# Attention backward for one query row: four stores of dV rewritten from 128 partitions to 124 and 4

## The chip, the core and the metric

The kernel runs on one core of a Trainium2 chip. The core has five engines with instruction streams of their own (PE for matrix products, DVE and ACT for elementwise work, POOL, and SP, which here only issues transfers) and sixteen DMA engines that carry all bytes between HBM and the on-chip memory of 128 partitions. The metric is device time in microseconds for one launch. Before the change it was 663.56 us, the median of 9 runs (662.63 to 664.14). Lower is better.

## What is computed

One query row per head attends to 8192 keys, for 32 heads of width 128. Output and the three gradients are wanted, all in bfloat16:

```python
B, H, Sq, Skv, Dh = 1, 32, 1, 8192, 128
scores = jnp.einsum('bhqd,bhkd->bhqk', q, k) * Dh ** -0.5
attn   = softmax(scores, axis=-1)
out    = jnp.einsum('bhqk,bhkd->bhqd', attn, v)
out, vjp = jax.vjp(forward, q, k, v); dq, dk, dv = vjp(grad_out)
```

K and V are 2 MB per head and are read once; dK and dV are 2 MB per head and are written once. Each row of dK is a number times q, and each row of dV is a probability times the gradient of the output, so both are outer products. In all 128 MB are read and 128 MB written.

## The kernel before

**Tiles.** A head's 8192 rows lie on 128 partitions with 64 consecutive rows each: partition p holds rows 64p to 64p + 63, 16 KB in one piece both in HBM and on chip. `rows_of(x, h, c, parts)` is the c-th of `parts` pieces of those 64 rows on every partition, and `slots(X, c, parts)` the same piece of a tile. A half (parts = 2) is 128 partitions of 8 KB, a quarter (parts = 4) 128 partitions of 4 KB. K has three buffers of a whole head, V two, and each of the two gradient tiles G two.

**Loop.** Iteration h works on head h and finishes head h - 1 beside it. For head h: four block transposes of K on DVE (line 142) and the scores on PE (line 154); maximum, exponential and sum (lines 262 to 289); then, on V, transposes on PE (line 180), their copies on ACT (line 182), the output product (line 197) and the products with the gradient (line 192). At its end `outer(h, "dv", r)` for r = 0 to 3 makes a quarter of dV each on DVE. For head h - 1 the same function makes the quarters of dK, spread over the iteration, and the gradient of q comes from K again (line 197).

**Stores.** `outer` multiplies on DVE (line 207) and, after every second quarter, issues the store of a half (line 215). For the last head it stores each quarter.

**Order of the transfers.** All transfers are issued by SP, and everything in the loop stands in an order written out by hand. In iterations 1 to 29 SP issues, in this order: V of the next head (line 81), the first half of dK of the previous head (line 215), K of the head after next (line 75), the second half of that dK, and the two halves of dV of this head: six transfers and 8 MB. The first K and V and the last V come in quarters.

**Waits.** SP waits before an issue for whatever the transfer needs: the tile's maker for a store, the last reader of the buffer for a load. It also waits for the landing of the transfer eight issues before, since eight completion semaphores are used in turn. Every transfer of 128 partitions is cut over the sixteen DMA engines, eight partitions on each, and it has landed when the last engine has finished its part.

Of the kernel before, what the change touches and what calls it, by code (L numbers as in the profile page):

```python
# [18 lines left out]
V_BUFS = 2  # L19
NST = 2  # L20
QD = 32


@with_exitstack
def kernel(
# [11 lines left out]
    nc = tc.nc  # L37
    P = 128
# [3 lines left out]
    NCH = NT // CH  # L42
    NQ = P // QD
    assert NCH == 4 and NQ == 4
    W = D // 2
    NB = W // QD
    scale = float(D) ** -0.5
# [15 lines left out]
    def rows_of(x, h, c, parts):  # L63
        L = NT // parts
        return x[0, h].rearrange("(p n) d -> p n d", p=P)[:, c * L:(c + 1) * L, :]

    def slots(X, c, parts):
        L = NT // parts
        return X[:, c * L:(c + 1) * L, :]
# [28 lines left out]
    nc.vector.reduce_sum(in_quad[:], ident[:].rearrange("p (a i) -> p a i", a=NQ), axis=AX.X)  # L98
    lane = consts.tile([P, QD], F32)
    nc.vector.reduce_sum(lane[:], ident[:].rearrange("p (a i) -> p i a", a=NQ), axis=AX.X)  # L100
# [3 lines left out]
    for w in range(NB):  # L104
        for e2 in range(2):
            four = consts.tile([H, NQ, QD], BF16, tag=f"four{w}{e2}")
            nc.vector.tensor_copy(
                four[:], rows[:, 0, :].rearrange("h (w j e) -> h w e j", w=NB, e=2)[:, w, e2:e2 + 1, :]
                .to_broadcast([H, NQ, QD]))
            tp = psT.tile([P, CH, P], BF16, tag="T")  # L110
# [26 lines left out]
    def k_blocks(h, u):  # L137


        if u == 0:  # L140
            XK[h] = ktpool.tile([P, CH, NB, NCH, QD], F32, tag="XK", name="XK_sb")
        nc.vector.transpose(XK[h][:, :, :, u, :],  # L142
# [57 lines left out]
    def outer(h, which, r):  # L200
        x = st[h]
        if r == 0:
            x[which] = gpool.tile([P, NT, D], BF16, tag=which, name="G_" + which)
        G, dst = x[which], out_2 if which == "dk" else out_3
        rep, row = x["ds"] if which == "dk" else x["p"], x["qd"][:, 0 if which == "dk" else 1, :]
        Q = NT // 4
        nc.vector.tensor_tensor(  # L207
            slots(G, r, 4).rearrange("p n (a b) -> p n a b", b=R),
            slots(rep, r, 4).unsqueeze(2).to_broadcast([P, Q, D // R, R]),
            row.rearrange("p (a b) -> p a b", b=R).unsqueeze(1).to_broadcast([P, Q, D // R, R]),  # L210
            op=ALU.mult)
        parts = 4 if h == H - 1 else NST
        if r % (4 // parts) == 4 // parts - 1:
            c = r // (4 // parts)
            nc.sync.dma_start(rows_of(dst, h, c, parts), slots(G, c, parts))

    def rows_bc(h):
        x = st[h]
# [21 lines left out]
    for h in range(H + 1):  # L240
# [8 lines left out]
        if h > 0:  # L249
            ds_of(p_)  # L250
            outer(p_, "dk", 0)
            dq_of(p_, 0)
# [3 lines left out]
        if h > 0:  # L256
            dq_of(p_, 1)
            outer(p_, "dk", 1)
# [11 lines left out]
        if h > 0:  # L270
            outer(p_, "dk", 2)
# [77 lines left out]
```

## Time and profile before

| | before |
|---|---|
| median of 9 runs | 663.56 us |
| the profiled execution | 663.56 us, of which its span 661.8 us |
| PE, PE weight load, DVE, ACT busy | 79%, 74%, 78%, 28% of the span |
| DMA | 408 GB/s on average; HBM read 134.23 MB, written 134.23 MB |
| stores of dV | 62 of 1024 KB (25.6 us from issue to landing), 4 of 512 KB |
| stores of dK | 62 of 1024 KB (27.8 us), 4 of 512 KB |
| loads of V | 30 of 2048 KB (28.2 us), 8 of 512 KB |

The span runs from the first to the last instruction of one execution; times in the chain of waits and in the windows count from its start. In the chain, each line is a start, a duration and the work that the next piece of the chain waited for. A transfer's duration there is from its issue to its landing, with the time that it waits behind others. The queue lines give packets, megabytes and the share of the sixteen engines' time. Queue 1 carries the kernel's transfers; queues 8 and 14 bring instructions.

### The profile page before, as it was taken

The numbers are of one execution on the slowest core, as the hardware profiler recorded it, in microseconds if no ns is written. First come the engines' busy times: TensorE is split into PE (matmuls) and PEld (weight loads), VectorE is DVE, ScalarE is ACT, GpSimd is POOL, SyncE is SP. The second block draws the span as 40 slices with busy tenths as digits, with TensorE's granted clock in tenths as the row PEclk, the third lists the DMA queues.
The fourth block names the chain that finished last, engine by engine and source line by source line (L and its number), as shares of the span: only waits on it lengthen the run. The fifth ranks groups of instructions, "written<-read, shape, count | busy, mean of one in ns | idle before, by whom it ended". The sixth has DMA issues, their size and how long they took to land.

```text
span 661.8 us, 21100 instructions
## 1 busy us (share of the span) xinstructions
PE 523.1 (79%) x9705; PEld 488.0 (74%) x9705; DVE 513.4 (78%) x664; ACT 182.2 (28%) x321; POOL 0.7 (0%) x6
## 2 busy tenths in 40 slices
PE   2888888789888778878778787788877888778880
PEld 1888788689887777877668776687766887667870
DVE  5789889788897797777977779777788776886862
ACT  0333223232333222232222322223222322222330
POOL 0000000000000000000000000000000000000000
PEclk9955556656565566655666556666566665566665
DMA  8999999999999999999999999999999999999783
GB/s 328 414 424 427 427 421 429 415 424 428 428 423 426 426 423 428 426 426 422 427 426 425 425 429 425 423 426 419 408 423 413 419 415 406 414 417 405 295 356 144
DMA packets 29800, 269.83 MB, mean 408 GB/s; under 512 B 3472, under 2 KB 3472, under 8 KB 6032
## 3 DMA queue, kind: packets, MB, share of 16 engines
q1 hardware_dynamic: 29712, 268.48, 97.2%
q8 instruction: 76, 1.25, 0.7%
q14 instruction: 12, 0.10, 0.0%
HBM read 134.23 MB, written 134.23 MB: 406 GB/s over the span
## 4 chain that ended last, share of the span: by engine, by line
DMA 70%; PE 21%; DVE 3%; ACT 2%; issue 1%; SPq 0%; ACTq 0%
DMA Kt<-in_k_dram 26%; DMA Vt<-in_v_dram 25%; DMA out_dram<-G_dv 19%; PE T_ps L180 9%; PE s_ps L154 2%; PE m_ps L197 2%; PE dp_ps L197 2%; PE dp_ps L192 2%; ACT XT_sb L182 1%; DVE XK_sb L142 1%; PE m_ps L267 1%; PE m_ps L280 1%; DVE G_dk L207 1%; ACT e L279 1%; PE s_ps L170 1%
## 5 line engine op out<-in xcount | busy, mean ns | idle before, releaser
L180 PE MATMUL T_ps<-ident_f,Vt 128*128 128x128 f32 x1024 | 240.0, 413 | 30.7 <-DMA Vt<-in_v_dram 30.7
L180 PEld LDWEIGHTS T_ps<-ident_f,Vt 128*128 128x128 f32 x1024 | 198.1, 221 | 31.9 <-issue 29.5
L142 DVE STREAM_TRANSPOSE XK_sb<-Kt 128x1024 f32<-128x1024 f32 x128 | 148.1, 1213 | 71.3 <-DMA Kt<-in_k_dram 71.3
L182 ACT COPY XT_sb<-T_ps 128x1024 f32<-128x1024 f32 x128 | 129.6, 1013 | 196.1 <-PE T_ps L180 196.1
L207 DVE TENSOR_TENSOR G_dk<-ds_rep,qd 128x2048 bf16<-128x2048 bf16 x128 | 155.7, 1218 | 1.1
L207 DVE TENSOR_TENSOR G_dv<-p_rep,qd 128x2048 bf16<-128x2048 bf16 x128 | 148.2, 1219 | 9.0 <-ACT p_rep L289 8.8
L192 PEld LDWEIGHTS <-XT_sb 128*128 128x128 bf16 x2048 | 76.6, 105 | 30.2 <-ACT XT_sb L182 27.5
L192 PE MATMUL dp_ps<-do_blk,XT_sb 128*128 128x2 bf16 x2048 | 72.9, 165 | 24.7 <-ACT XT_sb L182 24.7
L197 PE MATMUL dp_ps<-ds_rep,Kt 128*128 128x1 bf16 x2048 | 64.8, 165 | 6.5 <-issue 5.9
L197 PEld LDWEIGHTS <-Kt 128*128 128x128 bf16 x2048 | 60.0, 104 | 12.3 <-issue 12.2
L154 PE MATMUL s_ps<-q_blk,XK_sb 128*128 128x4 bf16 x2048 | 57.9, 167 | 10.4 <-DVE pdt L228 7.7
L154 PEld LDWEIGHTS <-XK_sb 128*128 128x128 bf16 x2048 | 55.4, 100 | 12.3 <-DVE pdt L228 9.4
L197 PEld LDWEIGHTS <-Vt 128*128 128x128 bf16 x2048 | 62.6, 106 | 2.0
L197 PE MATMUL m_ps<-p_rep,Vt 128*128 128x1 bf16 x2048 | 60.5, 166 | 0.0
L280 PEld LDWEIGHTS m_ps<-rs,ones_f 128*128 128x128 f32 x64 | 16.0, 310 | 48.6 <-ACT e L279 48.6
L280 PE MATMUL m_ps<-rs,ones_f 128*128 128x1 f32 x64 | 18.7, 362 | 39.2 <-ACT e L279 39.2
L238 ACT COPY dq_all<-dp_ps 128x1 f32<-128x1 f32 x32 | 5.1, 159 | 159.4 <-PE dp_ps L197 159.4
L276 DVE TENSOR_REDUCE nbias<-m_ps 128x1 f32<-128x128 f32 x32 | 9.3, 292 | 24.2 <-ACT qd L223 24.2
L230 DVE SCALAR_TENSOR_TENSOR ds_rep<-dp_ps,pdt,p_s 128x256 bf16<-128x256 f32 x32 | 15.5, 484 | 15.5 <-PE dp_ps L192 13.3
L267 PE MATMUL m_ps<-diag,ones_f 128*128 128x128 f32 x64 | 25.5, 499 | 2.2 <-issue 1.5
L289 ACT ACTIVATE p_rep<-e,rinv 128x256 bf16<-128x256 f32 x32 | 16.3, 508 | 30.2 <-DVE rinv L287 30.2
L223 ACT CAST qd<-m_ps 128x256 bf16<-128x256 f32 x32 | 11.9, 372 | 44.6 <-PE m_ps L219 44.6
(44 smaller groups left out, 161.4 us busy)
## 6 DMA issues: line engine op xcount, KB each, us to landing
Kt<-in_k_dram SPq DMA_DIRECT2D x31, 2048.0 KB, 27.8
out_dram<-G_dv SPq DMA_DIRECT2D x62, 1024.0 KB, 25.6
out_dram<-G_dk SPq DMA_DIRECT2D x62, 1024.0 KB, 27.8
Vt<-in_v_dram SPq DMA_DIRECT2D x30, 2048.0 KB, 28.2
Vt<-in_v_dram SPq DMA_DIRECT2D x8, 512.0 KB, 13.9
Kt<-in_k_dram SPq DMA_DIRECT2D x4, 512.0 KB, 5.4
out_dram<-G_dv SPq DMA_DIRECT2D x4, 512.0 KB, 16.8
out_dram<-G_dk SPq DMA_DIRECT2D x4, 512.0 KB, 11.1
```

Of the source, the lines that this page charges most:

```text
L142: nc.vector.transpose(XK[h][:, :, :, u, :], slots(Kt[h], u, NCH).rearrange("p g d -> p (g d)").bitcast(F32).rearrange("p (g w j) -> p g w ...
L154: nc.tensor.matmul(out[:, g, :], lhsT=cols[:, g, c // 2, c % 2], rhs=q_blk[:, h, c, :], start=(c == 0), stop=(c == 2 * NB - 1), skip_group ...
L180: nc.tensor.transpose(T_ps[:, i, :], words[:, m * P:(m + 1) * P], ident_f[:])
L182: nc.scalar.copy(X[:], T_ps[:])
L192: nc.tensor.matmul(st[h]["dp"][:, n:n + 2], lhsT=X[:, i, e2, :], rhs=do_blk[:, h, e2, :], start=(e2 == 0), stop=(e2 == 1), skip_group_chec ...
L197: nc.tensor.matmul(out_col, lhsT=Xt[:, n, :], rhs=rep[:, n, 0:1], start=(n == 0), stop=(n == NT - 1), skip_group_check=True)
L207: nc.vector.tensor_tensor(slots(G, r, 4).rearrange("p n (a b) -> p n a b", b=R), slots(rep, r, 4).unsqueeze(2).to_broadcast([P, Q, D // R, ...
L223: nc.scalar.copy(x["qd"][:].rearrange("p a d -> p (a d)"), x["m"][:, 256:512])
L230: nc.vector.scalar_tensor_tensor(out=x["ds"][:], in0=x["dp"][:, 0:NT].unsqueeze(2).to_broadcast([P, NT, R]), scalar=pdt[:], in1=x["p_s"][: ...
L267: nc.tensor.matmul(x["m"][:, 128:256], lhsT=ones_f[:], rhs=diag[:], start=True, stop=True, skip_group_check=True)
L280: nc.tensor.matmul(x["m"][:, 0:1], lhsT=ones_f[:], rhs=rs[:], start=True, stop=True, skip_group_check=True)
L289: nc.scalar.activation(x["p"][:], e[:].unsqueeze(2).to_broadcast([P, NT, R]), ACT.Copy, scale=rinv[:])
```

## The change

One branch is added to `outer`, for the second half of dV of heads 7, 13, 19 and 25. In place of one store of a half, three are issued: the third quarter on 128 partitions, then the last quarter of partitions 0 to 123, then the last quarter of partitions 124 to 127. The bytes and their places are the same. The products on DVE and their order are the same. According to its description, the last quarter's bytes move on DMA engines 0 to 3 alone.

```diff
+SHIFTED = (7, 13, 19, 25)
...
         parts = 4 if h == H - 1 else NST
         if r % (4 // parts) == 4 // parts - 1:
             c = r // (4 // parts)
-            nc.sync.dma_start(rows_of(dst, h, c, parts), slots(G, c, parts))
+            if which == "dv" and h in SHIFTED and c == 1:
+
+                nc.sync.dma_start(rows_of(dst, h, 2, 4), slots(G, 2, 4))
+                for lo, hi in ((0, P - 4), (P - 4, P)):
+                    nc.sync.dma_start(rows_of(dst, h, 3, 4)[lo:hi], slots(G, 3, 4)[lo:hi])
+            else:
+                nc.sync.dma_start(rows_of(dst, h, c, parts), slots(G, c, parts))
```

## The prediction

> **What bounds the kernel now.** I read the page first, then the chain of waits, then windows of the end, then the single packet records.
>
> ```profile
> span 661.8 us, 21100 instructions
> ...
> q1 hardware_dynamic: 29712, 268.48, 97.2%
> q8 instruction: 76, 1.25, 0.7%
> ...
> DMA 70%; PE 21%; DVE 3%; ACT 2%; issue 1%; SPq 0%; ACTq 0%
> ...
> Kt<-in_k_dram SPq DMA_DIRECT2D x31, 2048.0 KB, 27.8
> ```
>
> The sixteen DMA engines are busy 97.2% of the span, and a 2 MB load that needs 4.9 us at 427 GB/s lands 27.8 us after its issue: it waits behind other transfers. The chain of waits, in order of time, shows where that ends:
>
> ```profile
> 539.17 26.22 DMA out_dram<-G_dv
> 565.46 28.17 DMA Vt<-in_v_dram
> 593.69 27.77 DMA Kt<-in_k_dram
> 621.48 4.62 DVE XK_sb L142 x4
> ```
>
> Each transfer's landing lets SP issue the next, up to K of head 31 at 621.48; a fixed tail of about 40 us follows. So the time is set by when a transfer has landed on its *last* engine. The windows (length, busy time and count of PE, PEld, DVE, ACT, POOL, granted clock, DMA share, GB/s) show that one engine is last:
>
> ```profile
> 300.00:400.00 100.00, 79.84 (x1436) 74.39 (x1434) 77.09 (x97) 28.26 (x50) 0.00 (x0) 0.58 1.01 425
> ...
> 612.00:615.00 3.00, 1.39 (x6) 1.33 (x7) 2.37 (x5) 1.13 (x4) 0.00 (x0) 0.50 0.54 227
> ...
> 618.00:621.48 3.48, 3.48 (x33) 3.48 (x32) 1.09 (x1) 1.03 (x2) 0.00 (x0) 0.50 0.48 192
> ...
> 653.60:660.00 6.40, 0.00 (x0) 0.00 (x0) 0.00 (x0) 0.00 (x0) 0.00 (x0) 0.50 0.07 27
> ```
>
> Up to 600 us all are full. While K of head 31 is awaited half of the engines have nothing to do, and in the last 6.4 us the share is 0.07, one engine in sixteen, at 27 GB/s. The packet records carry no engine number, but an engine works its packets back to back (4 KB packets start 155 ns apart, 8 KB ones 306 ns, 16 KB ones 607 ns), so I linked each record's end to the next one's start, backwards from the end of the program. That gives sixteen sequences, each going through all transfers in SP's order, in three kinds:
>
> - One **laggard**, never idle from start to end, last on every transfer: about a quarter of its 8 KB store packets take 350 to 394 ns for 309, some 25 us in all.
> - Eight **interrupted** ones: the 76 instruction packets of q8 visit them in turn, nine or so each, 0.86 to 0.97 us each. They are ahead of the laggard by 11.1, 11.2, 13.5, 13.6, 14.1, 14.6, 16.3 and 16.4 us when K of head 31 lands.
> - Seven **free** ones, 19.1 to 20.4 us ahead there. Their lead at the last dV store of heads 7, 13, 19 and 25 is at least 6.1, 10.8, 15.9 and 18.6 us.
>
> **The change, part by part.** Removed: four stores of 1 MB, each 8 packets of 8 KB on every engine, 8 x 0.306 + 0.006 = 2.45 us. In the place of each:
> - 128 partitions x 4 KB: 8 x 0.155 + 0.006 = 1.25 us on all sixteen.
> - 124 x 4 KB: on four engines, as the change is worded, 31 partitions each: 31 x 0.155 + 0.006 = 4.81 us there.
> - 4 x 4 KB: one packet each, 0.16 us there.
>
> So twelve engines lose 2.45 - 1.25 = 1.20 us per shifted head, 4.8 us over four, and four engines get 1.25 + 4.81 + 0.16 - 2.45 = 3.77 us more to do, 15.1 us over four; the two groups move 4.97 us against each other at each head. The one-engine window checks the rate: 96 KB more at 27 GB/s are 3.6 us.
>
> That the four are numbers 0 to 3 is no reading of this trace. The Trainium skill (DMA: Bandwidth & Descriptors, Why a DMA increments its semaphore by 16 and not by 1) states that a transfer from SP runs on the largest number up to 16 that divides the outermost sizes, on the lowest-numbered engines: four for both 124 and 4; no row here shows such a transfer. The same page (Rules for kernel authors, Use all 16 engines) speaks against the edit; if all engines were equal, its rule would make the sum 663.6 + 15.1 = 678.7, where the laggard's row makes it 658.8.
>
> If the laggard is one of the twelve and the four stay ahead of it, the end comes 4.8 us sooner. With 16 of its quarter-slow 8 KB packets' worth gone as well (25 us / 992 packets = 0.025 us each), 5.2 at most.
>
> **Added on SP:** two more transfers per shifted head, eight in all, at 0.33 us of issue each (the row of a single store on SP's timeline): 2.6 us, hidden under waits of this kind, of which SP has hundreds of us:
>
> ```profile
> SPq L215 <- DMA Kt<-in_k_dram: 102.6, 25, 5.1
> SPq L215 <- DMA out_dram<-G_dk: 101.1, 50, 2.3
> ```
>
> A store shares no tile with a K load; it waits because SP has eight completion semaphores and each transfer takes that of the one eight before. Three short transfers for one therefore push two others out of the eight in flight: 10 to 11 MB outstanding become 8 to 9, of which the laggard's sixteenth is still some 18 us of work. Queued behind them are V and K loads, issued 2 to 5 us later than before; without the 18 us of cover those 5 us would come at each shifted head, 20 in all. The cover holds, so I cost it at nothing. The last store still waits for the same DVE product, which is made once per quarter as before. No instruction on PE, DVE or ACT changes.
>
> **Not shown: collisions.** After the edit an engine reads partitions that other engines read too. No row has two engines reading the same partitions. Lower bound 0, as in loads, which reach the partitions by writing. The nearest row for a disturbed store is the laggard's: (350 to 394)/309 is up to 1.27 times; the 24 additional packets' 3.7 us would become 4.7, 1.0 us per head, 4 in all. Above that, a full halving of the rate for 40% of the packets (each engine stores about half of its time) is 1.5 us per head, 6 in all. I take 0.5 per head, 2 in all, for the four; it matters only where the four set the end. The free engines have 1.1, 0.8 and 0.9 us left after the first three shifts (6.1 - 5.0, 10.8 - 9.9, 15.9 - 14.9, rounded) and -1.3 after the fourth (18.6 - 19.9), less what collisions take, but the eight-transfer limit had held them at 20 us for the last eight heads, in which the interrupted ones still won 2 to 5 us, so some of it comes back.
>
> **Forecast.** The four are free engines: 663.56 - 4.8 + 0.4 (a part of the collisions) = **659.2**; 658.2 to 662.0. The profiled execution took 663.56 with 1.8 around its span; the median of the nine runs is the same 663.56.
>
> **Rivals.**
> - *The four become the laggards.* Interrupted ones among the four lose 19.9 us against the laggard but are only 11.1 to 16.4 ahead. Followed to the end: K of head 31 landed on them 11 to 16 us early, +15.1, then 37.1 us of transfers and at most one 0.9 us fetch against the laggard's 39.1: -3.4 (16.4 ahead, no fetch) to +2.9 (11.1 ahead), about +0.3 for those of 13.5 to 14.1. With collisions of 2: 665.9; bounds 660.2 to 672.5. It decides when 19.9 plus collisions exceeds the four's lead by more than 4.8. For it: at the end, where fourteen engines start a store from idle, they start one after another within 0.15 us, and the engines that a fetch had just delayed leave every second slot empty (the twelfth, then the fourteenth of fifteen); if slots go by number, two of the first four are interrupted. Against: if slots alternate between a lower and an upper half, all of 0 to 3 may be free; the trace can't tell.
> - *The laggard is one of the four*: 663.56 + 15.1 = 678.7 (to 684.7 with collisions). By count 4 in 16; less, as the widest gap late in that order, 23 ns between the last two slots against 14 to 17 ns beside it, looks like the laggard's place, far from the first four.
> - *The bytes don't gather*: if 124 partitions spread over more engines than stated, little moves: 663.6, within 1.
>
> In a sentence by itself: the Trainium skill (same page, Latency and other measured facts) says that engines 7 and 15 are usually slower than the others, guessing at descriptor rings of GpSimd transfers; this kernel has none, yet one engine lags by 11.1 us, and were it 7 or 15, the second rival would fall and the time be 659.2 or 665.9.
>
> **How the numbers follow.** Forecast 0.48, first rival 0.36, second 0.10, third 0.06. About 0.2%, 1.3 us, is what a measurement of this kernel can tell from none. Faster: 0.47 of the forecast and 0.02 of the first rival, 0.49. Same: 0.01 + 0.10 + 0.05 = 0.16. Slower: 0.24 + 0.10 + 0.01 = 0.35. The range 657.8 to 668.5 leaves out the second rival and the first one's worst; the forecast's own is 658.2 to 662.0.
>
> **What would show it.** Issue rows of G_dv: 58 of 1024 KB, 8 of 512 KB, 4 of 496 KB, 4 of 16 KB. Forecast right: K of head 31 lands near 616.7, and the last microseconds still show a share of 0.06 to 0.07, one engine alone, ended sooner. First rival: K lands at 622 or later, and the share at the end is two to four sixteenths or the single laggard is another. Second: K near 636, one engine alone for over 20 us. Third: 496 KB issues land as fast as their neighbours of 512 KB. Wrong in any case if SP's waits move from landings to engines of compute, or if SP's issues take longer than 0.33 us.

## The result and the profile after

The changed kernel takes 660.77 us (median of 9 runs, 659.14 to 661.46) against 663.59 us for the kernel before (median of all its 29 runs, the nine of the table above among them). The ratio is 0.9957, with a 95% interval of 0.9949 to 0.9965: faster by 0.43%, or 2.8 us. The profiled execution took 659.26 us, 4.3 less than the profiled one of before; it is the second quickest of ten, so its trace shows more gain than the median has.

The page of the changed kernel: the span, the packets, the queues and the shares of the chain of waits.

```profile
span 657.5 us, 21116 instructions
...
DMA packets 30344, 269.83 MB, mean 410 GB/s; under 512 B 3504, under 2 KB 3504, under 8 KB 7088
...
q1 hardware_dynamic: 30256, 268.48, 97.8%
q8 instruction: 76, 1.25, 0.7%
...
DMA 61%; PE 28%; DVE 4%; ACT 3%; issue 2%; SPq 0%; ACTq 0%
```

The same line of packets in the kernel before:

```profile
DMA packets 29800, 269.83 MB, mean 408 GB/s; under 512 B 3472, under 2 KB 3472, under 8 KB 6032
```

The bytes are the same and the DMA engines are busier, 97.8% for 97.2%: there is less time in which some of them have nothing to do. Packets under 512 B went from 3472 to 3504. Of the 3472, 3344 are 4-byte packets, one for each of the sixteen engines in each of the 209 transfers: with it an engine reports that its part has landed, and the trace has the time of each such report. These times are called landings below. Three transfers for one would add 32 per head if all sixteen engines took part in each; the page shows 32 in all, 8 per head. Sixteen for the third quarter replace those of the half, so 8 are left for the two cut pieces: four engines each. In the linked packet records exactly four of the sixteen sequences carry the 31 + 1 additional packets, and the other twelve carry none. The bytes do gather.

The issues of the same kernel (source, queue, count, KB each):

```profile
out_dram<-G_dv SPq DMA_DIRECT2D x58, 1024.0 KB
...
out_dram<-G_dv SPq DMA_DIRECT2D x8, 512.0 KB
...
out_dram<-G_dv SPq DMA_DIRECT2D x4, 496.0 KB
out_dram<-G_dv SPq DMA_DIRECT2D x4, 16.0 KB
```

DVE's timeline of the changed kernel shows when K of head 31 has landed: its transposes on line 143 start then, and the bracket tells that DVE sat idle until the load. The second line is the kernel before.

```profile
617.41 4.62 DVE L143 STREAM_TRANSPOSE XK_sb<-Kt 128x1024 f32<-128x1024 f32 x4 [0.83 <-DMA Kt<-in_k_dram]
```

```profile
621.48 4.62 DVE L142 STREAM_TRANSPOSE XK_sb<-Kt 128x1024 f32<-128x1024 f32 x4 [2.40 <-DMA Kt<-in_k_dram]
```

The load landed 4.1 us sooner than before (its last report came at 617.39, against 621.46), and DVE's idle time before it is 0.83 us, where it was 2.40. The windows of the changed kernel (columns as in the prediction) show the other engines' waiting gone:

```profile
300.00:400.00 100.00, 82.06 (x1464) 76.57 (x1462) 78.05 (x98) 28.27 (x50) 0.00 (x0) 0.50 1.01 424
612.00:615.00 3.00, 3.00 (x72) 2.94 (x71) 3.00 (x3) 1.17 (x2) 0.00 (x0) 0.50 1.02 422
615.00:618.00 3.00, 3.00 (x30) 3.00 (x29) 2.17 (x3) 1.01 (x1) 0.00 (x0) 0.50 0.86 351
650.00:656.00 6.00, 0.00 (x0) 0.00 (x0) 0.00 (x0) 0.00 (x0) 0.00 (x0) 0.50 0.12 50
653.60:655.50 1.90, 0.00 (x0) 0.00 (x0) 0.00 (x0) 0.00 (x0) 0.00 (x0) 0.50 0.08 33
```

The middle of the program moves the bytes as fast as before (424 and 425 GB/s). Before, a share of 0.54 stood in 612 to 615; now all sixteen work until shortly before the load lands. At the end the share is again about one sixteenth: still one engine is alone, but for a shorter time. The chain of waits of the changed kernel (start, duration, work) has a new feature near the end:

```profile
545.27 25.84 DMA Vt<-in_v_dram
571.17 26.72 DMA Kt<-in_k_dram
597.91 4.62 DVE XK_sb L143 x4
...
622.40 1.62 PE s_ps L155 x64
```

The last load on it is K of head 30, and from there on it runs through the compute of heads 30 and 31, so PE's share rose from 21% to 28%. With K of head 31 in 4.1 us sooner, the compute before it ends 0.83 us ahead of the load: this wait is nearly used up.

The last report of the program comes at 656.55 us, against 660.84 before: 4.3 us sooner, where the relief of the laggard by plain count is 4.8. That last engine is the laggard again (its last stores take longer than the plain time, those of the next engine, 1.8 us ahead, don't). The four that got the bytes are all *free* engines. Their leads over the laggard at K of heads 10, 16, 22 and 28, after each shift, were 0.9 to 2.5, -0.2 to 2.9, -0.5 to 4.4 and -1.6 to 5.3 us. When K of head 31 lands, one of the four is the last, 0.3 us behind the laggard, and the other three are 2.1 to 7.4 us ahead of it (the remaining eleven engines 10.7 or more). So the change has used up the lead of the four to the last microsecond.

### The profile page after: what moved, and what is told of

It is laid out like the page before. It is cut to its first block, busy times and chain, and to the rows that moved or that the text cites. A ratio compares the mean times of both kernels' runs of the same rounds, so it can differ in the third digit from the quotient of the medians.

```text
span 657.5 us, 21116 instructions
## 1 busy us (share of the span) xinstructions
PE 521.6 (79%) x9705; PEld 486.4 (74%) x9705; DVE 513.5 (78%) x664; ACT 182.2 (28%) x321; POOL 0.7 (0%) x6
## 3 DMA queue, kind: packets, MB, share of 16 engines
q1 hardware_dynamic: 30256, 268.48, 97.8%
## 4 chain that ended last, share of the span: by engine, by line
DMA 61%; PE 28%; DVE 4%; ACT 3%; issue 2%; SPq 0%; ACTq 0%
DMA Kt<-in_k_dram 26%; DMA Vt<-in_v_dram 24%; DMA out_dram<-G_dv 12%; PE T_ps L181 11%; PE s_ps L155 4%; PE dp_ps L198 3%; PE m_ps L198 3%; DVE XK_sb L143 3%; PE dp_ps L193 2%; ACT XT_sb L183 2%; PE m_ps L274 1%; PE m_ps L287 1%; PE s_ps L171 1%; DVE G_dk L208 1%; ACT e L286 1%
## 5 line engine op out<-in xcount | busy, mean ns | idle before, releaser
L181 PE MATMUL T_ps<-ident_f,Vt 128*128 128x128 f32 x1024 | 237.4, 410 | 27.6 <-DMA Vt<-in_v_dram 27.6
L181 PEld LDWEIGHTS T_ps<-ident_f,Vt 128*128 128x128 f32 x1024 | 195.2, 218 | 28.6 <-issue 26.3
L155 PEld LDWEIGHTS <-XK_sb 128*128 128x128 bf16 x2048 | 56.5, 103 | 12.1 <-DVE pdt L235 8.6
L237 DVE SCALAR_TENSOR_TENSOR ds_rep<-dp_ps,pdt,p_s 128x256 bf16<-128x256 f32 x32 | 15.5, 484 | 14.2 <-PE dp_ps L193 12.1
```

The source lines that it names most:

```text
L155: nc.tensor.matmul(out[:, g, :], lhsT=cols[:, g, c // 2, c % 2], rhs=q_blk[:, h, c, :], start=(c == 0), stop=(c == 2 * NB - 1), skip_group ...
L181: nc.tensor.transpose(T_ps[:, i, :], words[:, m * P:(m + 1) * P], ident_f[:])
L237: nc.vector.scalar_tensor_tensor(out=x["ds"][:], in0=x["dp"][:, 0:NT].unsqueeze(2).to_broadcast([P, NT, R]), scalar=pdt[:], in1=x["p_s"][: ...
```

## The experiments

The theory is that of the forecast: engines with slack take bytes from the one that has none. Three things could be otherwise: that the gain comes from cutting as such, that the four are not what they seem, and that the collisions cost more than taken. Medians are of 4 to 12 runs, and numbers in brackets after a ratio are its 95% interval; each comparison is with runs of the kernel before on the same chip (663.43 us for 112 and 16 partitions, two heads, eight heads, and 120 and 8; 663.34 for the two portions, 119 and 9, and the two runs on packets; 663.02 for three heads, 125 and 3, and 126 and 2; 663.30 for the loads).

### The same cut without moving the bytes

```diff
-                for lo, hi in ((0, P - 4), (P - 4, P)):
+                for lo, hi in ((0, P - 16), (P - 16, P)):
```

> The same three stores at heads 7, 13, 19 and 25, but the last quarter cut at 112 and 16 partitions, so that all sixteen engines carry 7 and 1 packets of it. Theory (the gain is the laggard's relief of 1.20 us per shifted head, by bytes moved to four engines that are ahead): no byte changes engine, so 663.6, within 0.7. Rival (the gain comes from cutting the store in three, with shorter transfers in flight): the same gain as the change, about 660.8.

Measured: 665.17 us, 1.0020 [1.0010, 1.0031]. Both theories missed. The gain of the change doesn't come from cutting, and the version with the cut is 1.7 us slower (interval 0.7 to 2.1), 0.4 per head. The laggard carries as many bytes as before here. Its 4 KB packets in the four heads took 1.86 us more than they take undisturbed, but that isn't the loss: in the kernel before, the same bytes in 8 KB packets took 1.6 us more than undisturbed, by the landings. Compared transfer by transfer with the kernel before, the last landing gets 0.4 us later at the four cut places together. The profiled run is 1.5 us slower; the rest appears at other transfers, over half of it around head 25, and its cause isn't shown.

### Fewer heads, more heads

```diff
-SHIFTED = (7, 13, 19, 25)
+SHIFTED = (13, 25)
```

> The change at heads 13 and 25 alone. Theory: the laggard loses 2 x 1.20 = 2.4 us and stays the last engine, since the four lose about 2 x 5.6 us of a lead of 19 us; 661.2, and K of head 31 lands 2.4 us sooner than before, with one engine alone at the end. Rival (the four already set the end in most runs of the change, and each head costs them): two heads gain less than half of four, 662.2 or more.

Measured: 661.79 us, 0.9979 [0.9969, 0.9989]: 1.6 of the 2.4 us. At K of head 31 the laggard is last by 9.4 us over the nearest of the four, so here nothing but the laggard sets the time, and still 0.8 is missing. The landings of the profiled run (662.08) show where it isn't lost: set against the kernel before, the laggard's landing moves 1.45 us forward at the second half of dV of head 13 and 1.44 at that of head 25, more than the 1.20 of the plain count. It falls back by 0.4 us before head 13 and by about 1.0 between heads 24 and 25, where nothing is cut.

With heads 4, 7, 10, 13, 16, 19, 22 and 25:

> The change at eight heads, 4, 7, 10, 13, 16, 19, 22 and 25. Theory: the four engines become the last ones. They have 8 x (3.77 + 0.59 of disturbed packets) = 34.9 us more to do and are ahead by about 19 us, or 23 without the limit of eight transfers in flight, so the end comes 12 to 16 us later than before: 675 to 680. Rival (the four never bind, the gain per head goes on): 8 x 1.20 = 9.6 us less, 654.

Measured: 686.83 us, 1.0353 [1.0335, 1.0371]. The sign is right, the size was put too small. Windows of this run:

```profile
300.00:400.00 100.00, 68.28 (x1331) 63.66 (x1330) 68.72 (x87) 23.64 (x41) 0.00 (x0) 0.55 0.96 386
...
644.00:648.00 4.00, 4.00 (x35) 4.00 (x35) 2.98 (x3) 1.17 (x2) 0.00 (x0) 0.50 0.42 167
...
680.00:685.00 5.00, 0.00 (x0) 0.00 (x0) 0.00 (x0) 0.00 (x0) 0.00 (x0) 0.50 0.05 19
```

Already in the middle of the program the rate falls from 424 to 386 GB/s: engines wait for the last of the four. At K of heads 28 to 31, fourteen of the sixteen landings come 13 to 17 us before the last one. The last of the four had 11.1 us on top of the plain duration of its cut packets, the others 9.1, 3.3 and 3.3; the expectation had taken 0.59 per head, 4.7 us, for each.

With three heads, later in the program and seven apart:

```diff
-SHIFTED = (7, 13, 19, 25)
+SHIFTED = (10, 17, 24)
```

> The change at three heads, 10, 17 and 24. Theory (with four heads the laggard and the four are level, and the disturbed packets decide which of them ends a run): three heads take 3 x 1.20 = 3.6 us from the laggard, and the four stay some 5 us ahead, so 663.4 - 3.6 + 0.4 = 660.2, as good as four heads or better, and the slowest runs below 662. Rival (the laggard sets the end in all runs of the change and each head brings 0.7 us net, 2.8 / 4): 663.4 - 2.1 = 661.3.

Measured: 660.08 us (659.59 to 660.85), 0.9953 [0.9940, 0.9965], as expected. Its chain of waits:

```profile
561.61 28.10 DMA Vt<-in_v_dram
589.78 27.74 DMA Kt<-in_k_dram
617.54 4.62 DVE XK_sb L143 x4
```

Here the chain runs through K of head 31 again, since the laggard is the last on it, with the four 4.2, 9.0, 11.2 and 12.1 us ahead. Its landing moves forward by 1.45 to 1.49 us at each of the three shifted heads. Three heads bring 2.9 us and four bring 2.8: the fourth shift brings nothing. The intervals of the two versions overlap, so neither is shown to be the better one.

### The same bytes in two heads

The whole second half of dV of heads 13 and 24 is cut at 124, in packets of 8 KB:

```diff
-                nc.sync.dma_start(rows_of(dst, h, 2, 4), slots(G, 2, 4))
                 for lo, hi in ((0, P - 4), (P - 4, P)):
-                    nc.sync.dma_start(rows_of(dst, h, 3, 4)[lo:hi], slots(G, 3, 4)[lo:hi])
+                    nc.sync.dma_start(rows_of(dst, h, c, parts)[lo:hi], slots(G, c, parts)[lo:hi])
```

> At heads 13 and 24 alone, the whole second half of dV is cut at 124 and 4 partitions, in packets of 8 KB: as many bytes on engines 0 to 3 as in the change, with one added transfer in place of two at half as many heads, and no packet of 4 KB. Theory (cutting to 4 KB packets is what costs 0.3 us per head): the laggard loses 2 x 2.45 us and nothing is given back, 658.5, and engines 0 to 3, with 2 x 7.34 us more, stay some 5 us ahead at the end. Rival (a long burst on four engines disturbs the others, or their lead of 10.8 us at head 13 is spent by the 9.8): no better than the change, 660.8 or more.

Measured: 661.99 us, 0.9976 [0.9955, 0.9997], but from 658.88 to 664.97 in twelve runs. The best runs come near to what was expected, and the median is what the rival says. In the profiled run (660.38) one of the four is last at K of head 31, 3.2 us behind the next of the four and 4.2 behind the laggard. So in the traced run the four had become the last engines. That the same, by different amounts, makes the other runs slow fits their spread, but only this run has a trace.

### Which engine lags

The number of engines that a transfer uses changes with the partitions on which it lies. The Trainium skill (DMA: Bandwidth & Descriptors, Why a DMA increments its semaphore by 16 and not by 1) states that it is the largest divisor up to 16, and that these are the lowest-numbered engines. The count of packets under 512 B agrees for each cut tried here: 8 more per head for 124 and 4 (4 + 4), 23 for 120 and 8 (15 + 8), 16 for 119 and 9 (7 + 9), 16 for 126 and 2 (14 + 2), 8 for 125 and 3 (5 + 3), and 32 for 112 and 16 (16 + 16). That they are the lowest-numbered is the page's word; the four sets in which the laggard was found or not are nested as it says.

With 120 and 8, engine 15 alone is spared:

> The last quarter of the same four heads cut at 120 and 8 partitions. If such a transfer takes the largest number of engines up to 16 that divides its partitions, 120 go to engines 0 to 14 with 8 packets each, 8 to engines 0 to 7 with one, and engine 15 carries none. Theory A (the laggard is number 15): it loses the same 4 x 1.20 us as in the change, and no other engine has more than 0.2 us per head to add, so 663.6 - 4.8 = 658.8, below the change, and steadier. Theory B (the laggard has another number): nothing is taken from it, 663.6 to 664.2.

Measured: 665.59 us, 1.0032 [1.0019, 1.0044]. In the records the laggard carries 8 + 8 + 1 packets per shifted head, so it has a part in both cut pieces: one of the first eight, and not engine 15, which carries no cut piece at all. The landings agree: at head 25 the piece of 120 partitions lands last at 550.4 us and that of 8 at 550.6, the next engine on them at 537.9 and 538.1.

With 119 and 9:

> The last quarter of heads 7, 13, 19 and 25 cut at 119 and 9 partitions. By the same rule of the largest divisor, 119 go to engines 0 to 6 with 17 packets each and 9 to engines 0 to 8 with one each. Theory A (the laggard is number 7): it carries one packet in place of eight, 1.04 us less per head, 4.2 in all, and the cutting costs 0.3 us per head as in the run with 112 and 16 partitions: 660.3 to 660.9. Theory B (the laggard is 4, 5 or 6, which is what is left after the change and the run with 120 and 8): it carries ten packets more, 1.56 us per head, so 663.4 + 6.2 + 1.2 = 670.8.

Measured: 672.76 us, 1.0138 [1.0124, 1.0151]. A loss of 9.4 us says that the laggard is among the first seven, and the landings agree: at head 25 the pieces of 119 and 9 partitions land last at 556.4 and 556.6 us, the next engine on them at 546.7 and 546.9. As the laggard isn't among the first four, it is 4, 5 or 6.

With 125 and 3, five engines with 25 packets each:

> The last quarter of heads 7, 13, 19 and 25 cut at 125 and 3 partitions: engines 0 to 4 with 25 packets, 0 to 2 with one more. If the laggard is number 4: (8 + 25) packets of 0.155 us for 2.45 us, 2.7 us more per head, with disturbed packets 674 to 678. If it is 5 or 6: it loses 4.8 us as in the change, and the end is set by engines 0 to 4 with 11.4 us more to do: 659 to 663.

Measured: 678.11 us, 1.0224 [1.0210, 1.0238]. Its chain of waits:

```profile
579.82 28.19 DMA Vt<-in_v_dram
...
608.07 27.77 DMA Kt<-in_k_dram
...
635.87 4.62 DVE XK_sb L143 x4
```

and its windows:

```profile
630.00:636.00 6.00, 6.00 (x106) 5.93 (x105) 3.95 (x5) 2.19 (x3) 0.00 (x0) 0.54 0.55 186
668.00:676.00 8.00, 0.00 (x0) 0.00 (x0) 0.00 (x0) 0.00 (x0) 0.00 (x0) 0.50 0.06 22
```

K of head 31 comes 14.4 us later than before, and one engine alone works for the last 8 us. In the records that sequence has 25 packets in the large cut piece and none in the small one: at head 25 the piece of 125 partitions lands last at 562.3 us, 18 us after its next engine, and that of 3 partitions at 541.9. So it is 3 or 4, and 3 is one of the four of the change. **The laggard is engine number 4**, the first that the change spares. The run with 119 and 9 was on another chip than those with 120 and 8 and with 125 and 3, and fits the same number. This run is what the second rival would have looked like.

With 126 and 2:

> The same cut at 126 and 2 partitions: engines 0 to 5 with 21 packets, 0 and 1 with one more. If the laggard is number 6: it loses 4.8 us, and engines 0 to 5 with 8.2 us more to do stay ahead or level: 659 to 661. If it is 4 or 5: (8 + 21) x 0.155 - 2.45 = 2.06 us more per head, 8.2 in all, with disturbed packets 672 to 676.

Measured: 666.55 us, 1.0048 [1.0036, 1.0061]. The expectation stood on a wrong count: 126 is divisible by 14, and its packets lie on fourteen engines, nine on each. The laggard carries 8 + 9 packets of 4 KB there for 8 of 8 KB, 0.8 us over four heads by plain count. Its cut packets take 2.4 us more than undisturbed, where the uncut stores took 1.6 more in the kernel before, so some 2 of the 3.5 us aren't explained by what its packets do at the cuts. The landings narrow it down as well: at head 25 the piece of 126 partitions lands last at 551.0 us, that of 2 at 533.7, so the laggard is not one of the first two.

### Does the laggard lag by packets or by bytes?

From the kernel before, with dV of heads 0 to 30 in single transfers of 2 MB:

```diff
-        parts = 4 if h == H - 1 else NST
+        parts = 4 if h == H - 1 else 1 if which == "dv" else NST
```

> No engine is favoured; dV of heads 0 to 30 is stored in one transfer of 2 MB with packets of 16 KB in place of two halves with 8 KB packets. If the laggard's extra time is a fixed 25 to 35 ns per store packet, 31 x 8 packets fewer save 6 to 9 us: 655 to 657.5. If it goes with the bytes, nothing changes: 663.4, within 0.7.

Measured: 663.46 us, 1.0002 [0.9989, 1.0015]. Half as many packets of dV, and no difference. The laggard's loss on a transfer can be read from the landings: its last landing, less the last landing of the transfer before it, less the plain time of its packets on one engine. Summed over dV from 30 to 610 us, it is 16.4 us with 232 packets of 16 KB, and 16.4 with 464 of 8 KB in the kernel before: not half.

From the kernel before, with dV of all heads in quarters:

```diff
-        parts = 4 if h == H - 1 else NST
+        parts = 4 if h == H - 1 or which == "dv" else NST
```

> The reverse: dV of all heads stored in quarters with 4 KB packets. In both cases 31 x 0.09 = 2.9 us more for the shorter packets themselves. If the laggard's extra time is per packet: 31 x 16 packets more at 25 to 29 ns, 12 to 14 us, so 678 to 681. If it goes with the bytes: 666.3.

Measured: 667.21 us, 1.0060 [1.0048, 1.0072], an increase of 3.9 us, of which 2.9 are the plain additional time of smaller packets on one engine. The laggard's loss on dV is 15.9 us, on 912 packets of 4 KB. From 232 to 912 packets it doesn't grow: the laggard doesn't lag by packets. It doesn't lag by bytes alone either. In the kernel before, the median loss is 0.49 us on the second half of a head's dV and 0.19 on the first, 0.09 and 0.14 on the halves of dK, and nothing on the loads, for 1 MB in each store. A whole head's dV loses 0.66 in one transfer. What makes the second half of dV the costliest was not tested; it is the half that the change cuts. The run also says that 62 additional short transfers and 4 KB packets cost the change next to nothing (its four third quarters are such). That leaves the cut off the even eight partitions per engine for the 0.4 us per head of the 112 and 16 version, by elimination; the trace places only 0.1 of it at the cut.

### Loads in place of stores

From the kernel before: the same bytes are moved to the four engines, but as the last quarter of four loads of V.

```diff
+        if h in SHIFTED:
+            E = NT - NT // 4
+            src = v[0, h].rearrange("(p n) d -> p n d", p=P)
+            nc.sync.dma_start(Vt[h][:, :E, :], src[:, :E, :])
+            for lo, hi in ((0, P - 4), (P - 4, P)):
+                nc.sync.dma_start(Vt[h][lo:hi, E:, :], src[lo:hi, E:, :])
+            return
```

> From the kernel before, with the stores left alone: the load of V of heads 7, 13, 19 and 25 is cut instead, three quarters of its columns on 128 partitions (12 KB packets), the last quarter on 124 and on 4 partitions. The bytes that leave twelve engines and go to four are the same as in the change (1.2 us less per head there, 3.8 us more per head on the four). Theory A, the cost of a cut off the 128 partitions lies in stores, whose engines then read partitions that other engines read too: loads don't have it, the four keep some 2 us of lead over the laggard, and the whole 4.8 us shows but for a few tenths: 658.4 to 659.3. Theory B, any transfer cut off the 128 partitions pays some 0.4 to 0.6 us per head: 660.3 to 661.3, as the change. If the K or V landing is held up by the four themselves (a load sets the end of a wait directly, a store only through the order of the queues), it is above 661.5.

Measured: 662.14 us, 0.9980 [0.9971, 0.9989]: the third case, and theory A fell. Chain and windows of this run:

```profile
567.45 27.70 DMA Vt<-in_v_dram
...
595.21 26.72 DMA Kt<-in_k_dram
...
621.95 4.62 DVE XK_sb L150 x4
```

```profile
612.00:615.00 3.00, 1.30 (x5) 0.86 (x5) 2.04 (x5) 1.18 (x4) 0.00 (x0) 0.50 0.94 396
...
618.00:622.00 4.00, 4.00 (x47) 4.00 (x45) 1.81 (x3) 1.17 (x2) 0.00 (x0) 0.50 0.61 229
656.00:660.00 4.00, 0.00 (x0) 0.00 (x0) 0.00 (x0) 0.00 (x0) 0.00 (x0) 0.50 0.06 22
```

K of head 31 lands as late as before, at 621.9, on one of the four; the laggard is 3.4 us ahead of it. The cut load packets are disturbed more than the cut store packets: 1.48 us on top per engine and head (16 samples, 0.08 to 2.30), against 0.59 in the change (0 to 1.84), 196 of the 512 taking 200 ns or more, most often about 310, where 159 is plain. What the disturbance is, whether two engines in the same partitions or another effect of the cut, was not separated.

## Why the prediction was right, and where it was off

**The bound.** Right: one engine sets the time. Where engine 4 gets additional bytes (125 and 3: 8 + 25 packets of 4 KB for 8 of 8 KB, by the prediction's durations 2.7 us per head, 10.7 in all), the whole of them, and 4.4 us more, is seen in the time. Where engines 0 to 3 get them, nothing is seen until their lead is used up.

**The relief of 4.8 us.** Confirmed at the shifted heads, and nearly whole in the profiled run: the laggard's last landing came 4.3 us sooner, and K of head 31 landed 4.1 sooner. That this run took 659.26 us, and the forecast was 659.2, is luck: it is the second quickest of ten, and the median is 660.77. The laggard's excess (what its packets take above their undisturbed duration, up to 610 us) stays between 27.7 and 29.5 us in the kernel before, in the change and in the versions with two heads, three heads and cut loads, so the second saving that the prediction allowed for (0.025 us for each packet's worth, 5.2 in all) isn't visible in these sums, which differ by more from run to run. At the single heads it is: 1.44 to 1.49 us in place of 1.20 in the runs with two and three heads. It was taken too small there, as the bytes that were moved come from the half on which the laggard loses most.

**Who the four are.** Right, and the case was decided here. The reading that the widest gap in the start order marks the laggard "far from the first four" reached a right conclusion by a wrong reading: the laggard is number 4, next to them. Either that gap isn't the laggard's place or the order of starts from idle isn't the order of the numbers; no run tells which. The first rival's argument from slots came out wrong as well: none of the first four is an interrupted engine. In the 120 and 8 run, two of 5 to 7 and six of 8 to 14 are the interrupted engines; 0 to 3 and 15 are free.

**Collisions.** Taken at 0.5 us per head for the four; measured 0.59 above the undisturbed duration. The nearest row, the laggard's disturbed store, was a fair guide. The bound of nothing "as in loads, which reach the partitions by writing" was wrong: cut loads cost 1.48.

**The four stay ahead of the laggard.** This is the step that was mis-sized, as the term "+0.4 (a part of the collisions)". The profiled run has it (659.26 for 659.2), but the median has 2.0 in its place (4.8 - 2.8). Two parts of the runs bear on that. With two heads 0.8 us is missing and with three 0.7, in versions where the four are 4 to 9 us ahead in the trace, so that this part isn't theirs. Nor is it lost at the cuts, where the traces show more than the full relief; with three the interval (2.3 to 4.0 us gained) holds the full 3.6, with two (0.7 to 2.1) it falls 0.3 short of 2.4, and it isn't explained further. The additional 1.3 (2.0 in place of 0.7) appears with the fourth head, where the four are level with the laggard. There the later of two ends counts, and any disturbance of either is a loss; the trace shows the level in one run, and that it makes the loss in the others is argued from the spread (659.1 to 661.5; 658.9 to 665.0 with the bytes in two portions; 659.6 to 660.9 with three heads), not seen in their records.

**What would show it.** The four rows of issues came as written. K of head 31 landed at 617.4, forecast 616.7. The last microseconds have a share of 0.08, one engine with little beside it. Not foreseen: at the end of the chain compute of head 30 takes over from the load of head 31.

**SP.** Eight more transfers were costed at nothing, under SP's waits. The waits of SP in the changed kernel (total us, times, longest):

```profile
SPq L222 <- DMA out_dram<-G_dk: 91.4, 45, 2.3
SPq L222 <- DMA Kt<-in_k_dram: 85.3, 21, 4.5
...
SPq L220 <- DMA out_dram<-G_dv: 18.5, 8, 2.6
```

SP still waits for landings, and the cut stores on line 220 wait at most 2.6 us, for a store eight transfers before. No issue became the bound, and the run with all of dV in quarters says the same for 62 more transfers.

**The rule against the edit.** The Trainium skill (DMA: Bandwidth & Descriptors, Rules for kernel authors, Use all 16 engines) advises a transfer shape that uses all sixteen. If all engines were equal, leaving twelve out would have made the time 678.7, by the prediction's estimate. They are not equal: the measured 660.8 is what four engines with 20 us of slack allow. With eight heads that slack is spent, and the time is 686.8.

## What to carry to other kernels

Where DMA sets the time, ask for the last engine and not for the mean: a share of one sixteenth at the end and engines that wait together before each landing show it, and bytes can be taken from the last engine by cutting a transfer on a number of partitions that only other engines serve. Count the lead of the engines that receive the bytes and stop before it is used up: two heads gave 1.6 us, three 2.9, four 2.8, eight lost 23. A cut off the even division has a price of its own: 0.4 us per head in the time of the version with all sixteen engines, and on the four engines 0.6 us per half MB in stores and 1.5 in loads. So it pays only for an engine that is several microseconds late.

## What the runs showed of the hardware

- One DMA engine, number 4, is slow in stores on these runs: 23 to 24 us above the plain time of its stores of dK and dV between 30 and 610 us, with dV in packets of 4, 8 or 16 KB, and two thirds of that on dV.
- The Trainium skill (DMA: Bandwidth & Descriptors, Latency and other measured facts) names engines 7 and 15 as usually slower, and ties its guess at the cause to transfers issued from GpSimd, which this kernel doesn't have. Here 4 is the slow one and 15 is a free engine: sparing 15 alone made the kernel slower by 2.2 us.
- The instruction fetches on queue 8 (76 packets of 16 KB, 72 of them of 0.88 to 0.99 us, the others up to 1.31) fall on eight of the engines in turn, nine or ten on each, and not on 0 to 4 or 15.
- A transfer on 126 partitions used fourteen engines and one on 119 seven (counted by their reports of landing); the number of partitions decides the balance among engines, by its divisors.
